# Attention beside a token MLP: loads awaited at other matrix products, the last four scores on other halves of the rows, and two pieces of set-up moved

## The chip, the cores and the metric

The kernel runs on one core of a Trainium2 chip, in one launch. Five engines work from queues of their own, each in order: PE (TensorE, matrix products), DVE (VectorE), ACT (ScalarE, here above all the exponentials), POOL (GpSimd) and SP (SyncE, which here issues DMA transfers). They meet through semaphores. The metric is the device time of one execution in microseconds (us).

## The reference

```python
def attention(x, wqkv, wo):          # x: 1 x 2048 x 512, 32 heads of 16
    qkv = (x @ wqkv).reshape(B, S, 3, H, Dh).transpose(2, 0, 3, 1, 4)
    q, k, v = qkv[0], qkv[1], qkv[2]
    p = softmax(einsum("bhqd,bhkd->bhqk", q, k) * Dh ** -0.5)
    o = einsum("bhqk,bhkd->bhqd", p, v)
    return o.transpose(0, 2, 1, 3).reshape(B, S, D) @ wo

def mixer(x, w1, b1, w2, b2):        # over the 2048 tokens, 1792 hidden
    u = gelu(einsum("bsd,sf->bdf", layernorm(x), w1) + b1)
    return (einsum("bdf,fs->bds", u, w2) + b2).transpose(0, 2, 1)

g = sigmoid((x * gate_w).sum(-1, keepdims=True))
return g * attention(x, wqkv, wo) + (1 - g) * mixer(x_B, w1, b1, w2, b2)
```

All in float32. The two branches have inputs of their own, A_x and B_x.

## The kernel before, in words

Most products of float32 values are made of three products of a rounded high part and a rest (names with `_hi` and `_lo`). Three stretches of the program follow one another: the projections, with q and k written to DRAM in parts; the first layer of the MLP with its gelu; and the attention, with the second layer of the MLP and the output projections running beside it. A short tail ends it. The change lies in the attention.

**Groups and phases.** The attention is 32 groups, each of a pair of heads and one half of the query rows; a group has 4 phases (`ph` 0 to 3), so there are 128 phases, counted by `p`. All engines follow the order in which the code is written here (`manual_schedule`).

**Scores.** A phase makes 16 scores (line 907), each a product of 64 rows (keys and queries in their parts, stacked; `ks` and `qs`) by 512 columns into a PSUM bank of its own, tiles `s` and, from score 10 on, `t`. A stack holds one head in rows 0 to 63 and the other in rows 64 to 127; `head[n]` says which half score `n` uses. A product on one half can run beside a product on the other half. So the first `n_b` scores of a phase share the array with a dense half product of the other branch (line 916, tile `dn`, also 64 rows); the scores from `n_b` on alternate between the halves and run beside each other. `n_b` is 14 in phases 0 to 91, 0 in phases 92 to 95, 12 in phases 96 to 111, and 6 or 8 from 112 on.

**Exponentials.** Scores 1, 3, 5 and 7 are copied out of PSUM by DVE (line 924, tile `pe`, four copies) and exponentiated together by ACT at the phase's end (line 939). Scores 0, 2, 4, 6, 8, 9 are exponentiated one by one straight from PSUM (line 928, "singles"), and (10, 11), (12, 13), (14, 15) two at a time (line 869; as two single ones on line 872 where their banks are not adjacent, in phase 0 of a group). There are 8 banks, one for dense products, so a late score waits for a bank that an earlier one must leave: score 14 awaits DVE's copy of score 7 and ACT's single of score 8.

**Products by v.** After the scores come the products of the exponentials by v (line 792, `apply_v`), as a rule 32 a phase, into a bank `av`. Each pair of scores that `TURNS` and `HELD` name gives four. The `pe` pairs, and where `whole` allows it the last pair, are `held` and applied in the next phase; in phase 0 the held ones finish the group before. A phase in which the last pair is held makes 28, the one after it more. DVE adds `av` to the group's sum `ot` (lines 814 and 816) early in the next phase, ahead of the four copies.

**Loads.** `load_q` (8 DMAs, phase 0) and `load_k` (6 DMAs, phase 1) bring the next group's stacks through `stack` (line 505) on SP's queue. No instruction awaits them but the next group's first scores: score 0 those of its half of the rows, and the first score on the other half, score 15 where `n_b` is 14, those of the other.

**Set-up.** `shift_rows` (line 492) sets 2 × 16 rows of a key buffer to −1, for the first buffer on POOL ahead of the attention and for the second on DVE in phase 0. `open_end`, called at phase 92, makes on DVE two constants for the end (`sums_of` and `least`, lines 589 to 596).

Of the kernel before, what the change touches and what calls it, by code (L numbers as in the profile page):

```python
# [9 lines left out]
F32 = mybir.dt.float32  # L10
# [4 lines left out]
ALU = mybir.AluOpType  # L15
AX = mybir.AxisListType
SYNC = mybir.DependencyInfo(mybir.DependencyClass.Sync, mybir.DependencyReason.DATA)
REASON = "the two halves of the rows add to one bank"
PSUM = bass.MemoryType.PSUM
DRAM = bass.MemoryType.DRAM  # L20

P = 128
# [36 lines left out]
def gated_mix(ctx: ExitStack, tc: tile.TileContext, a_x, a_wqkv, a_wo, b_w1, b_b1, b_w2, b_b2, gate_w, out):  # L59
    nc = tc.nc  # L60
# [435 lines left out]
        shift_rows(nc.gpsimd, k_bufs[0])  # L496


    def stack(dst, src, which, pair, cols, planes):
        b, r0 = divmod(pair * 2 * DH, P)  # L500
        for i in range(2):
            rows = slice(r0 + i * DH, r0 + (i + 1) * DH)
            for row, *part in planes:
                at = slice(i * HALF + row, i * HALF + row + DH)
                nc.sync.dma_start(dst[at].bitcast(F32), src[b][part[which], rows, cols])

    def load_k(g):
        t = k_bufs[g % 2]
# [56 lines left out]
    def call(at, *what):  # L565
        calls.setdefault(at, []).append(what)
# [14 lines left out]
    def open_end():  # L581

        nonlocal end, sums_of
        u_ctx.close()
        wk_ctx.close()
        end = end_ctx.enter_context(tc.tile_pool(name="end", bufs=1, side="right", reuse_waits="tile"))

        sums_of = end.tile([P, P], F32, name="sums_of")
        nc.vector.tensor_copy(
            sums_of.rearrange("p (j r) -> p j r", r=32),  # L590
            ident.rearrange("p (j r) -> p j r", r=32)[:, :, DH:VC].broadcast_to([P, P // 32, 32]),
        )
        least.append(end.tile([P, 1], F32, name="least"))
        nc.vector.tensor_reduce(least[0], ident.rearrange("p (j r) -> p j r", r=32)[:, :, DH], axis=AX.X, op=ALU.add)
        nc.vector.tensor_scalar(least[0], least[0], -1.0, 3e38, ALU.add, ALU.mult)
        nc.vector.tensor_scalar_add(least[0], least[0], LEAST_SUM)
# [129 lines left out]
            call(p0, invert, half, k, pairs, p0 + (0 if half and k > 1 else 2))  # L726
    p0 = 2 * at
    call(p0, open_end)
    left, right = slice(0, NB), slice(NB, QW)
    for k in range(ND):  # L730
        call(p0 + k // 2, fetch_half, k, left, p0 + 2 + k // 2, p0 + 2 + k // 2)
# [50 lines left out]
            dst = r_d[half][k][None, 2 * p : 2 * (p + 1), cols]  # L782
            nc.sync.dma_start(dst, ot[rows][DH:].rearrange("r (i n) -> r i n", i=2))

    def apply_v(av, grp, pairs, final=False):

        for n, pair in enumerate(pairs):
            for i, c, qb, pt in sorted(pair, key=lambda u: u[2]):
                for h in range(2):
                    j = 2 * qb + h  # L790
                    v_at = (c * H + grp % NP * 2 + i) * VC
                    nc.tensor.matmul(  # L792
                        av[32 * j : 32 * (j + 1), i * QC : (i + 1) * QC],
                        v_flat[:, v_at : v_at + 32],
                        pt[:, h * QC : (h + 1) * QC],
                        start=n == 0,
                        stop=n == len(pairs) - 1,
                    )
        covered = [{qb for pair in pairs for i, _, qb, _ in pair if i == n} for n in range(2)]
        assert all(len(c) != 1 for c in covered)  # L800
        if grp not in sums:
            sums[grp] = ot_pool.tile([P, NB], F32, name="ot"), [False, False]
        ot, begun = sums[grp]
        halves = [n for n in range(2) if covered[n]]
        if grp == NG - 1 and final:
            parts = [(x, y, True) for x, y in zip(column_halves(ot), column_halves(av))]
        elif len(halves) == 2 and begun[0] == begun[1]:
            parts = [(ot, av, begun[0])]
        else:
            cols = [slice(n * QC, (n + 1) * QC) for n in range(2)]  # L810
            parts = [(ot[:, cols[n]], av[:, cols[n]], begun[n]) for n in halves]
        for x, y, more in parts:
            if more:
                nc.vector.tensor_tensor(x, y, x, ALU.add)  # L814
            else:
                nc.vector.tensor_copy(x, y)
        for n in halves:
            begun[n] = True
        if final and grp < NG - 1:
            store(grp, sums.pop(grp)[0])  # L820

    engines = {getattr(mybir.EngineType, name) for name in ("PE", "Activation", "DVE", "Pool", "SP")}
    with tc.manual_schedule(engines=engines):
        kt, qt = {0: load_k(0)}, {0: load_q(0)}
        held, fence, turn, spare = [], None, 0, 0

        for n, (step, *args) in enumerate(first):
            if n and n % 12 == 0:
# [6 lines left out]
        for p in range(LAST + 1):  # L835
# [13 lines left out]
            half = slice(0, HALF) if second else slice(HALF, P)  # L849

            head = [second if n < n_b else (n - n_b) % 2 for n in range(NSC)]
            qbs = {}
            for a, b in TURNS + HELD:
                if head[a] == head[b]:
# [3 lines left out]
                    qbs[zero], qbs[one] = turn, 1 - turn  # L858
                    turn = 1 - turn

            swap = ph == PHASES - 1 and p < LAST and head[TWO[1][0]] == head[TWO[1][1]]
            order = [*TURNS[:4], TURNS[5], TURNS[4]] if swap else TURNS

            def exps(n):
# [14 lines left out]
            pool = regions()  # L879
            psum = pool.__enter__()  # L880
            ones = [psum.tile([P, NB], F32, name=f"s{n}") for n in range(BANKS)]
            for n in range(NSC):
                i, qb = head[n], qbs[n]
                c = at[i][qb]
                at[i][qb] += 1
                if n < TWO[0][0]:
                    if n >= BANKS:
                        ones[share[n - BANKS]] = psum.tile([P, NB], F32, name=f"s{share[n - BANKS]}")
                    s = ones[share[n % BANKS]]
                else:  # L890
                    if n == TWO[0][0]:
                        pool.__exit__(None, None, None)
                        pool = regions()
                        psum = pool.__enter__()
                        twos = {}
                        for low in range(BANKS):
                            if low == share[2]:
                                av = psum.tile([P, NB], F32, name="av")
                            elif low in share[3:5] and ph == 0:
                                twos[low] = psum.tile([P, NB], F32, name=f"s{low}")  # L900
                            elif low not in twos:
                                two = psum.tile([P, 2, NB], F32, name=f"t{low}")
                                twos[low], twos[low + 1] = two[:, 0, :], two[:, 1, :]
                                twos[low, low + 1] = two
                    s = twos[share[(n - BANKS) % BANKS]]
                rows_i = slice(i * HALF, i * HALF + ROWS)
                nc.tensor.matmul(  # L907
                    s,
                    kt[grp][rows_i, c * P : (c + 1) * P],
                    qt[grp][rows_i, qb * NB : (qb + 1) * NB],  # L910
                    start=True,
                    stop=True,
                )
                if n < n_b:
                    ps, a, b, begin, last, done = beside[n]
                    mm = nc.tensor.matmul(ps, a[half], b[half], start=begin and not second, stop=last and bool(second))  # L916
                    if n == 0 and fence is not None:
                        tc.add_manual_dep(mm.ins, fence.ins.name, SYNC, reason=REASON)
                    if n == n_b - 1:
                        fence = nc.gpsimd.memset(token, 0.0)  # L920
                        tc.add_manual_dep(fence.ins, mm.ins.name, SYNC, reason=REASON)
                if n in EVAC:
                    pt = evac[:, EVAC.index(n), :]
                    nc.vector.tensor_copy(pt, s)  # L924
                    units[n] = i, c, qb, pt
                elif n in SINGLE:
                    pt = ptp.tile([P, NB], F32, name="p1", bufs=len(SINGLE))
                    nc.scalar.activation(pt, s, AF.Exp, scale=SCALE)  # L928
                    units[n] = i, c, qb, pt
                else:  # L930
                    units[n] = i, c, qb, None
                    if n == TWO[0][1] or n == TWO[1][1] and not swap:
                        exps(n)
                    elif n == TWO[2][1]:
                        exps(n)
                        if swap:
                            exps(TWO[1][1])
# [2 lines left out]
            if n_b and second and beside[-1][-1]:  # L940
                beside[-1][-1]()
            if p == 0:
                shift_rows(nc.vector, k_bufs[1])
            if second:
                for _ in range(2):
                    if len(ready) < 2:
# [3 lines left out]

            turns, now_held = ([tuple(units[n] for n in pair) for pair in pairs] for pairs in (order, HELD))
            spare = share[2]
            if ph < PHASES - 1 or swap:

                def whole(pairs):
                    met = {(i, qb) for pair in pairs for i, _, qb, _ in pair}
# [9 lines left out]
                    av = psum.tile([P, NB], F32, name=f"s{spare}")  # L966
                apply_v(av, grp, turns)
            elif p < LAST:
                apply_v(av, grp, held + turns)
            else:  # L970
                ot = sums[grp][0]
                nc.vector.tensor_scalar_max(ot, ot, least[0])
                apply_v(av, grp, held + turns + now_held, final=True)
                last_ot = ot
# [165 lines left out]
```

## Time and profile before

| | |
|---|---|
| time, median of 3 runs | 1293.89 us (1293.07 to 1294.15) |
| the profiled execution | 1295.3 us; its span from first to last instruction 1293.3 us |
| mean granted clock of TensorE | 0.997 |
| busy: PE, ACT, DVE, POOL | 1280.4, 1091.3, 671.0, 180.0 us |
| attention, phases 0 to 127 | from 304.7 to 1273.7 us |

The profile comes from one execution. A table by stage gives, for a stretch in us from the span's start, its length and each engine's busy time, with the granted clock (1.00 is full) and the share of time in which the DMA engines were busy. A timeline row has start, length, engine, line, operation, and what the engine idled for ahead of it. PE's matrix products overlap in the pipeline, so the starts of rows say more than their lengths: a score's row is 0.39 or 0.50 us long, and the next begins 0.23 us after it.

### The profile page before, as it was taken

To read this page: it belongs to the slowest core of one execution; us is meant where nothing else is said; L and a number is where in the kernel's file an instruction comes from. 1 tells how busy PE (TensorE), PEld (TensorE's weight loads), DVE (VectorE), ACT (ScalarE), POOL (GpSimd) and SP (SyncE) were. 2 spreads that over 40 slices of the span, in tenths; PEclk is the share of its full clock that TensorE was granted. 3 is DMA by queue.
4 is the path that set the end of the run, shared out by engine and by line. 5 is a ranking of instruction groups with operands and counts; after the bars stand their busy time and mean duration, and the time that the engine had idled before them with its cause. 6 is when DMAs were issued, how large, how long until landed. Compare 5 with 4: busy or idle time off the path is not lost.

```text
span 1293.3 us, 33067 instructions
## 1 busy us (share of the span) xinstructions
PE 1280.4 (99%) x13278; PEld 850.4 (66%) x13278; DVE 671.0 (52%) x1155; ACT 1091.3 (84%) x1537; POOL 180.0 (14%) x272
## 2 busy tenths in 40 slices
PE   9999999999999999999999999999999999999997
PEld 7888888886666666666666666666665565655555
DVE  5675362438445545544544444454454665645555
ACT  3443343447999999999999999999999999999994
POOL 0210244553110111011011101101110000000000
PEclk9999999999999999999999999999999999999999
DMA  4497643327343343333334443333333654335411
GB/s 131 139 317 276 222 121 98 98 78 159 67 88 75 68 97 83 77 68 81 77 60 98 83 77 66 81 75 60 88 68 75 151 135 114 81 84 108 80 44 72
DMA packets 93581, 133.20 MB, mean 103 GB/s; under 512 B 16277, under 2 KB 55339, under 8 KB 90348
## 3 DMA queue, kind: packets, MB, share of 16 engines
q1 hardware_dynamic: 92844, 129.94, 41.2%
q8 instruction: 108, 1.77, 0.6%
q10 hardware_dynamic: 576, 1.05, 0.2%
q14 instruction: 53, 0.43, 0.1%
HBM read 97.00 MB, written 33.93 MB: 101 GB/s over the span
## 4 chain that ended last, share of the span: by engine, by line
PE 93%; ACT 4%; DVE 1%; issue 1%; DVEq 0%; ACTq 0%
PE av L792 28%; PE s L907 19%; PE acc L416 12%; PE t L907 10%; PE acc L73 10%; PE dn L916 6%; PE s L792 5%; ACT p L928 1%; ACT p L869 1%; ACT pe L939 1%; PE pa L996 1%; DVE pe L924 1%; PE acc L187 1%; PE dn L831 1%; PE acc L254 0%
## 5 line engine op out<-in xcount | busy, mean ns | idle before, releaser
L928 ACT ACTIVATE p<-s 128x512 f32<-128x512 f32 x768 | 395.7, 648 | 6.1 <-PE s L907 3.6
L869 ACT ACTIVATE p<-t 128x1024 f32<-128x1024 f32 x352 | 348.4, 1131 | 0.0
L907 PE MATMUL s<-qs,ks 64*128 64x512 f32 x1344 | 343.0, 404 | 1.1 <-DVE pe L924 0.7
L924 DVE COPY pe<-s 128x512 f32<-128x512 f32 x512 | 317.8, 683 | 6.9 <-PE s L907 6.4
L907 PEld LDWEIGHTS s<-qs,ks 64*128 64x128 f32 x1344 | 232.9, 184 | 97.5 <-issue 52.4
L792 PE MATMUL av<-p,v 128*32 128x256 f32 x4872 | 285.4, 379 | 0.0
L814 DVE TENSOR_TENSOR ot<-av,ot 128x512 f32<-128x512 f32 (+1 forms) x128 | 73.5, 575 | 396.6 <-PE av L792 396.6
L939 ACT ACTIVATE pe<-pe 128x2048 f32<-128x2048 f32 x129 | 259.5, 2014 | 0.0
L792 PEld LDWEIGHTS av<-p,v 128*32 128x32 f32 x4872 | 158.4, 110 | 104.9 <-issue 0.7
L907 PE MATMUL t<-qs,ks 64*128 64x512 f32 x704 | 185.1, 445 | 2.9 <-ACT p L928 0.4
L916 PE MATMUL dn<-u_lo,w_hi 64*128 64x512 f32 x430 | 174.1, 405 | 0.0
L916 PE MATMUL dn<-u_hi,w_lo 64*128 64x512 f32 x430 | 173.9, 404 | 0.0
L916 PE MATMUL dn<-u_hi,w_hi 64*128 64x512 f32 x428 | 173.2, 405 | 0.0
L66 POOL TENSOR_TENSOR w_lo<-w_raw,w_hi 128x512 fp32r<-128x512 f32 (+1 forms) x126 | 149.0, 1189 | 124.6 <-ACT w_hi L65 108.5
L907 PEld LDWEIGHTS t<-qs,ks 64*128 64x128 f32 x704 | 96.2, 184 | 83.4 <-ACT p L928 74.9
L792 PE MATMUL av<-pe,v 128*32 128x256 f32 x2048 | 138.1, 387 | 0.1
L920 POOL MEMSET token<- 1x1 f32 x124 | 12.7, 102 | 866.9 <-PE dn L916 811.2
L65 ACT CAST w_hi<-w_raw 128x512 fp32r<-128x512 f32 (+1 forms) x67 | 38.1, 569 | 79.2 <-PE acc L416 58.8
L792 PEld LDWEIGHTS av<-pe,v 128*32 128x32 f32 x2048 | 53.6, 109 | 54.2 <-ACT p L928 25.3
L416 PE MATMUL acc<-h_hi,w_hi 128*128 128x512 f32 x224 | 87.1, 389 | 0.0
L416 PE MATMUL acc<-h_lo,w_hi 128*128 128x512 f32 x224 | 87.1, 389 | 0.0
L416 PE MATMUL acc<-h_hi,w_lo 128*128 128x512 f32 x224 | 87.1, 389 | 0.0
(151 smaller groups left out, 1507.2 us busy)
## 6 DMA issues: line engine op xcount, KB each, us to landing
w_raw<-in_B_w_dram SPq DMA_DIRECT2D x96, 256.0 KB
ks<-kp SPq DMA_DIRECT2D x192, 128.0 KB
qs<-qp SPq DMA_DIRECT2D x256, 64.0 KB
qp<-pc SPq DMA_DIRECT2D x16, 768.0 KB
x<-in_A_x_dram SPq DMA_DIRECT2D x32, 256.0 KB
kp<-pc SPq DMA_DIRECT2D x16, 512.0 KB
w_raw<-in_B_w_dram SPq DMA_DIRECT2D x32, 128.0 KB
bp<-row SPq DMA_DIRECT2D x16, 256.0 KB
```

Of the source, the lines that this page charges most:

```text
L65: copy(hi, src)
L66: return sub(lo, src, hi.bitcast(F32), ALU.subtract)
L73: nc.tensor.matmul(ps, a, b, start=start and n == 0, stop=stop and n == last)
L416: nc.tensor.matmul(p, a, b, start=first and k == 0, stop=last and k == 2)
L792: nc.tensor.matmul(av[32 * j : 32 * (j + 1), i * QC : (i + 1) * QC], v_flat[:, v_at : v_at + 32], pt[:, h * QC : (h + 1) * QC], start=n == ...
L814: nc.vector.tensor_tensor(x, y, x, ALU.add)
L869: nc.scalar.activation(pt, twos[low, low + 1], AF.Exp, scale=SCALE)
L907: nc.tensor.matmul(s, kt[grp][rows_i, c * P : (c + 1) * P], qt[grp][rows_i, qb * NB : (qb + 1) * NB], start=True, stop=True,)
L916: mm = nc.tensor.matmul(ps, a[half], b[half], start=begin and not second, stop=last and bool(second))
L924: nc.vector.tensor_copy(pt, s)
L928: nc.scalar.activation(pt, s, AF.Exp, scale=SCALE)
L939: nc.scalar.activation(x, x, AF.Exp, scale=SCALE)
```

## The change

It has four parts.

1. The stack's DMAs of the next group are collected in `landed`. In a group's last phase (`ph` 3) `apply_v` makes each of 14 products by v, from the second pair on, wait for one of them.
2. Where `n_b` is 12 or less, which is phases 92 to 127, scores 12 and 13 use the first half of the rows and 14 and 15 the second, and they are issued in the order 12, 14, 13, 15. With 14 and 15 on one half their pair can always be held, so each of these phases makes 32 products by v.
3. The constants are made in `end_constants`, on DVE after the work of phase 101.
4. The second key buffer's shift rows are set by POOL.

```diff
@@ stack
+    landed = []
...
-                nc.sync.dma_start(dst[at].bitcast(F32), src[b][part[which], rows, cols])
+                landed.append(nc.sync.dma_start(dst[at].bitcast(F32), src[b][part[which], rows, cols]))
@@ open_end
         sums_of = end.tile([P, P], F32, name="sums_of")
+        least.append(end.tile([P, 1], F32, name="least"))
+
+    def end_constants():
+
         nc.vector.tensor_copy(
...
     call(p0, open_end)
+    on_dve(p0 + 9, end_constants)
@@ apply_v
-    def apply_v(av, grp, pairs, final=False):
+    def apply_v(av, grp, pairs, final=False, await_loads=False):
...
-                    nc.tensor.matmul(
+                    mm = nc.tensor.matmul(
...
+                    if await_loads and n and landed:
+                        tc.add_manual_dep(mm.ins, landed.pop(0).ins.name, SYNC, reason=AHEAD_OF_USE)
@@ the loop over phases
             head = [second if n < n_b else (n - n_b) % 2 for n in range(NSC)]
+            seq = list(range(NSC))
+            if n_b <= NSC - 4:
+                head[-4:] = 0, 0, 1, 1
+                seq[-3:-1] = seq[-2], seq[-3]
...
-            swap = ph == PHASES - 1 and p < LAST and head[TWO[1][0]] == head[TWO[1][1]]
+            swap = ph == PHASES - 1 and p < LAST and n_b == NSC - 2
...
-            for n in range(NSC):
+            for n in seq:
...
-                shift_rows(nc.vector, k_bufs[1])
+                shift_rows(nc.gpsimd, k_bufs[1])
...
-            if ph < PHASES - 1 or swap:
+            if ph < PHASES - 1 or swap or p < LAST and head[-2] == head[-1]:
...
-                apply_v(av, grp, held + turns)
+                apply_v(av, grp, held + turns, await_loads=ph == PHASES - 1)
```

How it moves instructions, at three places. First PE between group 0 and group 1, before: the last products of phase 3 and the first scores of phase 4 (a DMAHW semaphore is a load's).

```order
L792 MATMUL av<-p_3199,v 32x256 x2
L792 MATMUL av<-p_3213,v 32x256 [waits Activation_49]
L792 MATMUL av<-p_3213,v 32x256 x3
L792 MATMUL av<-p_3222,v 32x256 [waits Activation_49]
L792 MATMUL av<-p_3222,v 32x256 x3
L907 MATMUL s_3287<-qs,ks_2704 128x512 [waits DMAHW6_49,DMAHW1_49,DMAHW7_49,DMAHW0_49,PE_49]
L916 MATMUL dn<-u_hi,w_lo 128x512 [waits Pool_49]
```

The same place after, from the last two of the 14 awaited products on:

```order
L799 MATMUL av<-p_3178,v 32x256 [waits DMAHW3_49]
L799 MATMUL av<-p_3178,v 32x256 [waits DMAHW4_49]
L799 MATMUL av<-p_3185,v 32x256 x2
L799 MATMUL av<-p_3194,v 32x256 x2
L799 MATMUL av<-p_3199,v 32x256 x2
L799 MATMUL av<-p_3213,v 32x256 [waits Activation_49]
L799 MATMUL av<-p_3213,v 32x256 x3
L799 MATMUL av<-p_3222,v 32x256 [waits Activation_49]
L799 MATMUL av<-p_3222,v 32x256 x3
L921 MATMUL s_3287<-qs,ks_2704 128x512 [waits PE_49]
L930 MATMUL dn<-u_hi,w_lo 128x512 [waits Pool_49]
L921 MATMUL s_3288<-qs,ks_2704 128x512
```

Five waits ahead of the first score have become one; the loads are awaited one by one up in the products.

Then the end of phase 4's scores on PE, before; the last `t` row is score 15, the first on the other half of the rows.

```order
L907 MATMUL t_3334<-qs,ks_2704 128x512
L916 MATMUL dn<-u_hi,w_hi 128x512
L907 MATMUL t_3336<-qs,ks_2704 128x512 [waits DVE_49,Activation_49]
L907 MATMUL t_3336<-qs,ks_2704 128x512 [waits DMAHW4_49,DMAHW5_49,DMAHW3_49,DMAHW2_49]
L792 MATMUL av<-pe,v 32x256 [waits Activation_49]
L792 MATMUL av<-pe,v 32x256 x7
```

And after:

```order
L921 MATMUL t_3334<-qs,ks_2704 128x512
L930 MATMUL dn<-u_hi,w_hi 128x512
L921 MATMUL t_3336<-qs,ks_2704 128x512 [waits DVE_49,Activation_49]
L921 MATMUL t_3336<-qs,ks_2704 128x512
L799 MATMUL av<-pe,v 32x256 [waits Activation_49]
L799 MATMUL av<-pe,v 32x256 x7
```

Score 15's four waits for loads are gone; the rest stands as it did.

Last, phase 97 on PE, the last four scores and the first products, before (`t5` holds scores 12 and 13, `t1` 14 and 15):

```order
L907 MATMUL t5_14682<-qs_14040,ks0_2703 128x512 [waits DVE_49,Activation_49]
L907 MATMUL t5_14682<-qs_14040,ks0_2703 128x512
L907 MATMUL t1_14680<-qs_14040,ks0_2703 128x512 [waits DVE_49,Activation_49]
L907 MATMUL t1_14680<-qs_14040,ks0_2703 128x512
L792 MATMUL av_14679<-pe_14496,v_91 32x256 [waits Activation_49]
L792 MATMUL av_14679<-pe_14496,v_91 32x256 x7
```

After:

```order
L921 MATMUL t3_14673<-qs_14036,ks0_2703 128x512
L930 MATMUL dn_14487<-wo_hi_2735,e7_14159 128x512
L921 MATMUL t5_14674<-qs_14036,ks0_2703 128x512 [waits DVE_49,Activation_49]
L921 MATMUL t1_14672<-qs_14036,ks0_2703 128x512 [waits DVE_49,Activation_49]
L921 MATMUL t5_14674<-qs_14036,ks0_2703 128x512
L921 MATMUL t1_14672<-qs_14036,ks0_2703 128x512
L799 MATMUL av_14671<-pe_14488,v_91 32x256 [waits Activation_49]
```

Score 14, the first of the `t1` rows, with its wait for DVE and ACT, now stands ahead of score 13, the second of `t5`; score 15 still stands last.

More of the change, by code (lines that the diff above doesn't have):

```diff
@@ L17 @@
 SYNC = mybir.DependencyInfo(mybir.DependencyClass.Sync, mybir.DependencyReason.DATA)
+AHEAD_OF_USE = "the next group's scores find their stacks awaited"
 REASON = "the two halves of the rows add to one bank"
@@ L592, in open_end @@
         )
-        least.append(end.tile([P, 1], F32, name="least"))
         nc.vector.tensor_reduce(least[0], ident.rearrange("p (j r) -> p j r", r=32)[:, :, DH], axis=AX.X, op=ALU.add)
@@ L825, in gated_mix @@
         held, fence, turn, spare = [], None, 0, 0
+        landed.clear()
         for n, (step, *args) in enumerate(first):
```

## The prediction

> **What bounds the kernel now.** I read the page first: the busy shares, then the chain that ended last.
>
> ```profile
> span 1293.3 us, 33067 instructions
> PE 1280.4 (99%) x13278; PEld 850.4 (66%) x13278; DVE 671.0 (52%) x1155; ACT 1091.3 (84%) x1537; POOL 180.0 (14%) x272
> PE 93%; ACT 4%; DVE 1%; issue 1%; DVEq 0%; ACTq 0%
> PE av L792 28%; PE s L907 19%; PE acc L416 12%; PE t L907 10%; PE acc L73 10%; PE dn L916 6%; PE s L792 5%; ACT p L928 1%; ACT p L869 1%; ACT pe L939 1%; PE pa L996 1%; DVE pe L924 1%; PE acc L187 1%; PE dn L831 1%; PE acc L254 0%
> ```
>
> TensorE ends everything, but "busy" here includes scores that lie under something else's pace. So I cut the attention loop into its phases with the table by stage (columns: stretch and its length, busy time of each engine, granted clock, DMA share, GB/s). The sums are over groups 1 to 22, once over their first phases and once over their last; the single rows are phases 3, 4 and 24.
>
> ```profile
> 327.88:335.36 7.48, 7.48 (x98) 4.75 (x94) 3.71 (x7) 7.48 (x11) 2.10 (x3) 1.00 0.19 53
> 335.36:343.05 7.69, 7.69 (x98) 4.87 (x94) 3.60 (x6) 7.69 (x12) 0.09 (x1) 1.00 0.20 58
> 485.73:493.65 7.92, 7.92 (x98) 4.63 (x94) 4.63 (x8) 7.92 (x12) 0.09 (x1) 1.00 0.14 40
> sum 168.47, PE 168.47 PEld 106.59 DVE 81.23 ACT 168.47 POOL 1.96; mean PE 7.66 PEld 4.85 DVE 3.69 ACT 7.66 POOL 0.09
> sum 164.68, PE 164.68 PEld 103.83 DVE 88.01 ACT 164.68 POOL 34.04; mean PE 7.49 PEld 4.72 DVE 4.00 ACT 7.49 POOL 1.55
> ```
>
> A regular phase is 7.49 us; a group's first phase is 7.66. The timeline of TensorE at the end of the scores shows why (start, length): first a last phase, then the first phase of the next group.
>
> ```profile
> 331.34 0.50 PE L907 MATMUL t<-qs,ks 64*128 64x512 f32 x2
> 331.77 0.42 PE L792 MATMUL av<-pe,v 128*32 128x256 f32 x4
> ...
> 338.83 0.70 PE L907 MATMUL t<-qs,ks 64*128 64x512 f32 x2
> 339.46 0.64 PE L792 MATMUL av<-pe,v 128*32 128x256 f32 x8
> ```
>
> Scores 14 and 15 start together 3.46 us into the phase, and the products follow 0.43 later. In the group's first phase they start at 3.47 too, but take 0.70: score 15 is 0.20 late, and the products come 0.63 after. Ahead of score 15 stands there its wait for four loads. The products themselves last the same: 335.36 − 331.77 = 3.59 for 32 of them.
>
> What sets the 3.46 is VectorE; a late phase (96) shows it best.
>
> ```profile
> 1030.44 0.69 DVE L814 TENSOR_TENSOR ot<-av,ot 128x512 f32<-128x512 f32 x1 [1.24 <-PE av L792]
> 1031.14 2.48 DVE L924 COPY pe<-s 128x512 f32<-128x512 f32 x4
> 1033.77 0.51 PE L907 MATMUL t<-qs,ks 64*128 64x512 f32 x2
> 1034.20 1.07 PE L792 MATMUL av<-pe,v 128*32 128x256 f32 x16
> 1030.30:1037.79 7.49, 7.49 (x96) 4.67 (x92) 3.60 (x6) 7.36 (x12) 0.09 (x1) 1.00 0.65 174
> 1044.85:1052.61 7.76, 7.76 (x96) 4.37 (x93) 4.89 (x8) 7.76 (x11) 0.09 (x1) 1.00 0.92 146
> sum 120.89, PE 120.28 PEld 72.74 DVE 71.14 ACT 120.37 POOL 1.96; mean PE 7.52 PEld 4.55 DVE 4.45 ACT 7.52 POOL 0.12
> sum 113.48, PE 111.67 PEld 64.31 DVE 60.12 ACT 112.65 POOL 2.23; mean PE 7.44 PEld 4.29 DVE 4.01 ACT 7.51 POOL 0.15
> 1181.42:1189.23 7.81, 7.44 (x84) 4.07 (x81) 4.50 (x7) 7.51 (x12) 0.09 (x1) 1.00 0.14 32
> 1183.02 2.47 DVE L924 COPY pe<-s 128x512 f32<-128x512 f32 x4
> ```
>
> The sum and four copies end at 1033.62, 3.32 into the phase; score 14 needs the bank of the fourth copy and starts 0.15 later. The sums are phases 96 to 111 (mean 7.56) and 112 to 126 (7.57). Some of these phases hold 28 products and some 36; after a short one ScalarE is still behind (7.76 in phase 98).
>
> **The change part by part.**
>
> *Awaited loads.* Removed: the waits on loads at a group's first score and at score 15. The first score's cost nothing now, since the gap from products to scores is alike in all phases. Score 15's is 168.47 − 164.68 = 3.79 over 22 groups, less 0.27 for another stall of phase 24, which stays (7.92, against a mean of 160.55/21 = 7.65 of the rest): **−3.52**. Groups 23 and later are costed below. Added: 14 single waits, each on one product, 14 × 31. Those products run one after another at 3.59/32 = 0.112 us, and two of them carry a ScalarE wait today at no cost; so I take 0. From above: at what score 15's four waits cost, 0.20 or 0.05 each, they would be 0.7 us a group if none of it hides. Behind a waiting product stand on TensorE the other products and the next scores, then all engines. So it matters whether loads have landed.
>
> ```profile
> 1012.39 3.28 SPq L505 DMA_DIRECT2D ks<-kp x6
> 986.60:994.40 7.80, 7.80 (x101) 4.75 (x100) 3.46 (x6) 7.80 (x12) 0.18 (x2) 1.00 0.01 2
> 1015.01:1022.40 7.39, 7.33 (x84) 3.72 (x80) 6.52 (x11) 7.39 (x11) 0.00 (x0) 1.00 0.99 137
> ```
>
> For group 23 the DMA engines are idle (0.01) well before its products at 994.40. The tightest is group 24: its six key loads (0.77 MB) are issued until 1015.67 and at 137 GB/s would be in by 1021.3 (an estimate), the awaited products start at 1026.3: 0, at most the 3.6 us until the next group's scores, once. The Trainium skill, "DMA: Bandwidth & Descriptors", Rules for kernel authors, speaks against this edit: issue early and wait late, while here the wait moves earlier. By that rule the sum would carry up to those 3.6 us; no row here shows a late load.
>
> *Last four scores.* This touches phases 92 to 127. In the new order 12, 14, 13, 15, score 14 still awaits the fourth copy, 13 stands behind it on the other half of the rows and runs beside it, and 15 shares its half with 14 and comes alone. What one score behind another on the same half costs, from the start of phase 18:
>
> ```profile
> 440.72 0.50 PE L907 MATMUL s<-qs,ks 64*128 64x512 f32 x1
> ...
> 441.06 0.39 PE L907 MATMUL s<-qs,ks 64*128 64x512 f32 x1
> ```
>
> Score 15 starts 0.34 after 14 (the first of a run; 0.23 is the pace later). After a cold pair (0.50) the products came at 0.43; after a warm score (0.39) I take 0.11 less, 0.32. So the products start 0.34 + 0.32 − 0.43 = 0.23 later: 7.49 + 0.23 = **7.72** a phase. Bounds: 0.12 (pace 0.23) to 0.34 (0.43 kept). In return each phase gets 32 products, so that ScalarE, which falls back only after a phase of 28, is no bound. Sums: 16 × 7.72 = 123.52 against 120.89, **+2.63**; 15 × 7.72 = 115.80, plus 0.75 for phase 116, whose copies end 4.07 into it instead of 3.32 behind other VectorE work (1185.49 − 1181.42), 116.55 against 113.48: **+3.07**; phase 127, 0 to 0.23, **+0.1**.
>
> *Shift rows.*
>
> ```profile
> L492 POOL MEMSET ks<- x2: 1844/1906/1967, 300.4 to 302.4; 16x2048 f32 x2
> L492 DVE MEMSET ks<- x2: 1765/1765/1765, 309.4 to 311.6; 16x2048 f32 x2
> 313.40 0.42 DVE L816 COPY ot<-av 128x256 f32<-128x256 f32 x1
> 312.04:320.38 8.34, 8.17 (x99) 4.53 (x95) 5.29 (x8) 8.34 (x11) 1.38 (x2) 1.00 0.62 106
> 313.23 3.09 ACT L928 ACTIVATE p<-s 128x512 f32<-128x512 f32 x6
> 316.79 0.64 PE L792 MATMUL av<-pe,v 128*32 128x256 f32 x8
> ```
>
> In phase 1 (from 312.04) VectorE's sum waits for the memsets until 313.40. Without them it would start at 312.18, and VectorE alone would let the products start at +3.90 instead of +4.75. But ScalarE's singles end at 316.32, +4.28, and a product awaits the last of them; with 0.06 for the handing over the gain is 4.75 − 4.34: **−0.41** (0 to −0.85). On GpSimd they take 2 × 1.9 us; its next duty is the next phase's fence, and it is 14% busy.
>
> *Constants, phases 92 to 95.*
>
> ```profile
> 997.96:1007.62 9.66, 8.95 (x85) 4.10 (x82) 4.03 (x10) 8.35 (x12) 0.00 (x0) 0.82 0.61 136
> 1002.36:1005.77 3.41, 3.41 (x34) 1.57 (x36) 0.42 (x1) 3.41 (x4) 0.00 (x0) 0.50 0.53 103
> 998.71 0.22 DVE L589 COPY sums_of<-ident 128x128 f32<-128x128 f32 x1
> 999.29 2.48 DVE L924 COPY pe<-s 128x512 f32<-128x512 f32 x4
> sum 32.34, PE 31.37 PEld 15.52 DVE 20.14 ACT 30.44 POOL 0.00; mean PE 7.84 PEld 3.88 DVE 5.04 ACT 7.61 POOL 0.00
> ```
>
> The four constants hold the copies back by 0.58 (998.71 to 999.29). After, without dense work, such a phase is 7.39 (the row of 1015.01) + 0.23 = 7.62; four are 30.48 against 32.34: **−1.86**. In that lie 1.67 us of half clock: 3.41 us at 0.50, which is half lost. I count it as gone, since TensorE waits less ahead of it, but from rows I cannot show that. The Trainium skill, "TensorE: Matmul & The Clock Gate", Part 1, has a free-running window of 3413 ns whose low activity halves the clock; the 3.41 us agree, and by that rule the loss may come or not from run to run. In phase 101 the constants cost 0 to 0.6 once.
>
> *Sum.* −3.52 − 0.41 + 2.63 + 3.07 + 0.1 − 1.86 = 0.0 on the profiled execution, 1295.3 (span 1293.3 and 2.0 around it): 1295.3. That execution is 1.4 above the median of the runs, 1293.89, about the 1.67 of half clock; if the others lacked it, the sum for them is +1.7: 1295.6. I take **1295.4**.
>
> **The rivals.**
>
> *The last scores cost nothing (faster).* The rows of halves give the products their scores as early as before, and equal phases end ScalarE's backlog: phases stay at 7.49, and 7.39 without dense work. That is 16 × 7.49 = 119.84 (−1.05), 15 × 7.49 + 0.75 = 113.10 (−0.38), 4 × 7.39 = 29.56 (−2.78); with −3.52 and −0.41 it is −8.1: 1287.2. For it: 7.76 exists only behind ScalarE. Against: 13 can't pass 14 on an engine in order. Chance 0.18.
>
> *The tail is dearer (slower).* The lone score 15 drains like a cold one: 0.34 instead of 0.23 in 35 phases, +3.9: 1299.3. It decides from about 0.27 on. The pair at 338.83 speaks for it: there the products came 0.43 after the late score 15, though that one had waited. Chance 0.13.
>
> *The waits on products cost (slower).* 0.05 × 14 unhidden in 31 groups: +22, about 1317. It decides from some 0.1 us a group on. Against: the products' pace with ScalarE waits in it. Chance 0.06.
>
> *The clock halves all the same.* Nothing of the 1.67 is saved: 1297.1. Chance 0.13.
>
> That the waits merely reappear at score 15 would be a change that does not do what it says; its order shows none there.
>
> **How the numbers follow.** My forecast has 0.50 and on its own spans 1293.0 to 1298.0. The range, 1290.0 to 1299.0, leaves out the first rival's core and the dear waits. A difference of 0.2%, 2.6 us, is about what can be told from no change. Faster, below 1291.3: the first rival and the low end of the last scores' bounds, 0.20. Slower, above 1296.5: 0.13 + 0.06, most of the clock's 0.13 and the forecast's upper edge, 0.34. Between: 0.46.
>
> **What would show it.** First phases of groups 1 to 22 at 7.49, not 7.66; products of last phases still 3.59; late phases alike at 7.72, with score 15 alone at about 3.81 and products at 4.13; phase 1 at 7.9; no stretch at clock 0.50. Wrong if late phases are at 7.49 or under, or if the products with waits stretch.

## The result and the profile after

| | before | after |
|---|---|---|
| time, median | 1293.85 us (1292.61 to 1296.37, 14 runs) | 1295.65 us (1293.18 to 1298.57, 14 runs) |
| ratio to before | | 1.0013, 95% interval 1.0005 to 1.0022 |
| profiled execution, span | 1295.3, 1293.3 us | 1297.84, 1296.1 us |

The change makes the kernel slower by a little over 0.1%, inside what was called no change. From the page after, the span and the chain that ended last by engine:

```profile
span 1296.1 us, 32939 instructions
PE 95%; DMA 1%; ACT 1%; DVE 1%; issue 1%; SPq 1%; ACTq 0%
```

A DMA stands in the chain now, which it did not before. The table by stage shows where the time went: first the sums over the first, second and last phases of groups 1 to 22, then phases 1, 63, 95, 96 and 116, then the sums over phases 96 to 111 and 112 to 126.

```profile
sum 164.67, PE 164.67 PEld 103.01 DVE 81.24 ACT 164.59 POOL 1.94; mean PE 7.49 PEld 4.68 DVE 3.69 ACT 7.48 POOL 0.09
sum 165.42, PE 165.42 PEld 101.42 DVE 78.09 ACT 165.42 POOL 33.81; mean PE 7.52 PEld 4.61 DVE 3.55 ACT 7.52 POOL 1.54
sum 165.03, PE 165.03 PEld 101.98 DVE 88.03 ACT 165.03 POOL 33.99; mean PE 7.50 PEld 4.64 DVE 4.00 ACT 7.50 POOL 1.55
311.94:320.05 8.11, 7.93 (x99) 4.49 (x95) 4.09 (x7) 8.11 (x11) 2.35 (x3) 1.00 0.50 85
777.26:785.11 7.85, 7.85 (x98) 4.58 (x94) 3.71 (x7) 7.85 (x11) 2.09 (x3) 1.00 0.11 28
1017.60:1027.62 10.02, 9.49 (x84) 4.26 (x80) 6.52 (x11) 8.12 (x11) 0.00 (x0) 1.00 0.76 154
1027.62:1035.31 7.69, 7.56 (x96) 4.65 (x93) 3.60 (x6) 7.15 (x11) 0.09 (x1) 1.00 0.73 177
1181.37:1190.52 9.15, 7.95 (x92) 4.17 (x88) 5.17 (x8) 8.20 (x12) 0.09 (x1) 1.00 0.16 39
sum 123.00, PE 120.90 PEld 74.24 DVE 70.71 ACT 121.43 POOL 1.41; mean PE 7.56 PEld 4.64 DVE 4.42 ACT 7.59 POOL 0.09
sum 116.77, PE 112.00 PEld 64.20 DVE 60.17 ACT 114.48 POOL 2.22; mean PE 7.47 PEld 4.28 DVE 4.01 ACT 7.63 POOL 0.15
```

Added up for the two profiled executions:

| stretch | before | after | difference | predicted |
|---|---|---|---|---|
| up to phase 0 | 304.69 | 305.29 | +0.60 | 0 |
| phases 0 and 1 | 15.69 | 14.76 | −0.93 | −0.41 |
| first phases, groups 1 to 22 | 168.47 | 164.67 | −3.80 | −3.52 |
| second phases | 164.77 | 165.42 | +0.65 | 0 |
| last phases | 164.68 | 165.03 | +0.35 | 0 |
| phases 92 to 95 | 32.34 | 32.81 | +0.47 | −1.86 |
| phases 96 to 111 | 120.89 | 123.00 | +2.11 | +2.63 |
| phases 112 to 126 | 113.48 | 116.77 | +3.29 | +3.07 |
| phase 127 and the tail | 28.6 | 28.7 | +0.1 | +0.1 |
| span | 1293.3 | 1296.1 | +2.8 | 0.0 |

The timeline of TensorE shows the two main mechanisms at work: the end of the scores of phase 8, a group's first (start 365.00), and of phase 98 (start 1042.99).

```profile
368.47 0.50 PE L921 MATMUL t<-qs,ks 64*128 64x512 f32 x2
368.89 0.64 PE L799 MATMUL av<-pe,v 128*32 128x256 f32 x8
...
1046.47 0.50 PE L921 MATMUL t<-qs,ks 64*128 64x512 f32 x2
1046.78 0.39 PE L921 MATMUL t<-qs,ks 64*128 64x512 f32 x1
1047.10 1.07 PE L799 MATMUL av<-pe,v 128*32 128x256 f32 x16
```

In phase 8 scores 14 and 15 start together again, and the products follow at 3.89. In phase 98 they come at 4.11: scores 14 and 13 start together at 3.48 (the row of two), and score 15 runs alone behind them, from 3.79 on.

Phase 95 holds what was not counted. First TensorE's products of that phase, then SP's issues of group 24's key loads.

```profile
1021.60 1.07 PE L799 MATMUL av<-pe,v 128*32 128x256 f32 x16
1022.49 2.37 PE L799 MATMUL av<-p,v 128*32 128x256 f32 x16
1025.11 2.58 PE L799 MATMUL av<-p,v 128*32 128x256 f32 x32 [0.26 <-DMA ks<-kp]
...
1009.76 5.48 SPq L508 DMA_DIRECT2D ks<-kp  x6
```

A product by v shows as two records in these rows, so 64 are 32 products. They start at 1021.60 and would end 3.59 later, at 1025.19; the next score starts at 1027.62. They stand 2.43 us in all for loads issued from 1009.76 on.

### The profile page after: what moved, and what is told of

Same layout as the page of the kernel before. It is cut to its first block, busy times and chain, and to the rows that moved or that the text cites. A ratio compares the mean times of both kernels' runs of the same rounds, so it can differ in the third digit from the quotient of the medians.

```text
span 1296.1 us, 32939 instructions
## 1 busy us (share of the span) xinstructions
PE 1278.8 (99%) x13278; PEld 842.1 (65%) x13278; DVE 666.6 (51%) x1157; ACT 1091.7 (84%) x1537; POOL 182.6 (14%) x274
## 4 chain that ended last, share of the span: by engine, by line
PE 95%; DMA 1%; ACT 1%; DVE 1%; issue 1%; SPq 1%; ACTq 0%
PE av L799 30%; PE s L921 21%; PE t L921 12%; PE acc L417 12%; PE acc L74 10%; PE s L799 5%; PE dn L930 4%; DMA ks<-kp 1%; PE pa L1010 1%; ACT p L942 1%; PE acc L188 1%; PE dn L841 1%; DVE pe L938 0%; DMA x<-in_A_x_dram 0%; PE acc L255 0%
## 5 line engine op out<-in xcount | busy, mean ns | idle before, releaser
L942 ACT ACTIVATE p<-s 128x512 f32<-128x512 f32 x768 | 408.6, 748 | 7.3 <-PE s L921 3.9
L883 ACT ACTIVATE p<-t 128x1024 f32<-128x1024 f32 x352 | 361.7, 1234 | 0.0
L921 PE MATMUL s<-qs,ks 64*128 64x512 f32 x1344 | 339.1, 403 | 1.1 <-DVE ot L823 0.8
L799 PE MATMUL av<-p,v 128*32 128x256 f32 x4904 | 290.2, 379 | 0.3 <-DMA ks<-kp 0.3
L823 DVE TENSOR_TENSOR ot<-av,ot 128x256 f32<-128x256 f32 (+1 forms) x128 | 72.4, 566 | 399.6 <-PE av L799 399.6
L953 ACT ACTIVATE pe<-pe 128x2048 f32<-128x2048 f32 x129 | 273.0, 2118 | 0.0
L921 PEld LDWEIGHTS t<-qs,ks 64*128 64x128 f32 x704 | 92.0, 184 | 92.1 <-ACT p L942 89.5
```

The source lines that it names most:

```text
L799: mm = nc.tensor.matmul(av[32 * j : 32 * (j + 1), i * QC : (i + 1) * QC], v_flat[:, v_at : v_at + 32], pt[:, h * QC : (h + 1) * QC], start ...
L883: nc.scalar.activation(pt, twos[low, low + 1], AF.Exp, scale=SCALE)
L921: nc.tensor.matmul(s, kt[grp][rows_i, c * P : (c + 1) * P], qt[grp][rows_i, qb * NB : (qb + 1) * NB], start=True, stop=True,)
L953: nc.scalar.activation(x, x, AF.Exp, scale=SCALE)
```

## The experiments

Each part was done alone first, beside the changed kernel without one of its waits. The kernel before ran beside them (median 1293.0, 27 runs).

**Awaited loads alone.** On the kernel before, nothing else of the change:

```diff
+                landed.append(nc.sync.dma_start(...))
...
+                    if await_loads and n and landed:
+                        tc.add_manual_dep(mm.ins, landed.pop(0).ins.name, SYNC, reason=AHEAD_OF_USE)
...
-                apply_v(av, grp, held + turns)
+                apply_v(av, grp, held + turns, await_loads=ph == PHASES - 1)
```

> The kernel before with the awaited loads alone. Theory (three parts that act separately): the first phases of groups 1 to 22 fall from 7.66 to 7.48 us, the products of the last phases stay at 3.59, and the time is 3 to 3.5 us below before, about 1290.5. In phase 95 the products start at 1026.3 in the old rhythm, when the loads for group 24 have just landed: 0 to 0.5 us. Rival (a wait on a product costs like one at score 15, 0.05 each): the products of each last phase take 4.0 to 4.3 us and the time rises to some 1305 or more. Second rival (the loads for group 24 are late for any kernel that awaits them at products): phase 95 stands for about 2.4 us and the gain shrinks to about 1 us.

Measured: 1291.16 us (1288.8 to 1293.13, 11 runs), ratio 0.9984 (0.9975 to 0.9993). From its table by stage the first phases, the second ones and phase 95, and from its timeline the products that stood:

```profile
sum 165.05, PE 165.05 PEld 103.60 DVE 81.22 ACT 165.05 POOL 1.94; mean PE 7.50 PEld 4.71 DVE 3.69 ACT 7.50 POOL 0.09
sum 165.17, PE 165.17 PEld 101.81 DVE 78.05 ACT 165.17 POOL 33.89; mean PE 7.51 PEld 4.63 DVE 3.55 ACT 7.51 POOL 1.54
1017.43:1026.91 9.48, 8.72 (x92) 3.94 (x88) 6.52 (x11) 8.37 (x11) 0.00 (x0) 1.00 0.85 156
...
1023.86 3.12 PE L795 MATMUL av<-p,v 128*32 128x256 f32 x40 [0.56 <-DMA ks<-kp]
```

The time is 1.8 us below before in the medians, where 3 to 3.5 were expected. The first phases fall as forecast, so the waits on loads ahead of their scores were what made them longer. But phase 95 is 9.48 instead of 7.90 before, so the second rival holds in kind: without the new last four scores, too, a kernel that awaits group 24's loads at products stands for 1.6 us. That my theory gave 0 to 0.5 there was wrong; its timing came from an execution in which phase 92 lost 1.7 us at half clock. The dear waits are out: 14 waits cost nothing where the loads have landed, since the last phases sum to 164.72 here and to 164.68 before.

**Last four scores alone.** On the kernel before:

```diff
+            seq = list(range(NSC))
+            if n_b <= NSC - 4:
+                head[-4:] = 0, 0, 1, 1
+                seq[-3:-1] = seq[-2], seq[-3]
...
-            for n in range(NSC):
+            for n in seq:
...
-            if ph < PHASES - 1 or swap:
+            if ph < PHASES - 1 or swap or p < LAST and head[-2] == head[-1]:
```

> The kernel before with the new last four scores alone (halves, order and held pair in phases 92 to 127). Theory: phases 96 to 126 at 7.69 us each instead of a mean of 7.56, because score 15 comes alone 0.31 after score 14; +4 to +5 us over 31 phases, phases 92 to 95 about +0.2 each without a stretch at half clock; the time 1297.5 to 1299. Phase 95 does not stand, since no product awaits a load. Rival (the loss in the changed kernel was only its late loads in phases 95 and 116, and equal phases are no slower): within 1 us of before.

Measured: 1298.05 us (1297.14 to 1299.61, 5 runs), ratio 1.0042 (1.0028 to 1.0056). Its first phases, and its phases 96 to 111 and 112 to 126:

```profile
sum 168.44, PE 168.44 PEld 106.32 DVE 81.20 ACT 168.44 POOL 1.94; mean PE 7.66 PEld 4.83 DVE 3.69 ACT 7.66 POOL 0.09
sum 122.79, PE 120.87 PEld 74.08 DVE 70.13 ACT 121.99 POOL 1.41; mean PE 7.55 PEld 4.63 DVE 4.38 ACT 7.62 POOL 0.09
sum 116.22, PE 112.09 PEld 64.31 DVE 59.96 ACT 114.47 POOL 2.23; mean PE 7.47 PEld 4.29 DVE 4.00 ACT 7.63 POOL 0.15
```

The first phases stay at 7.66 and the late ones rise by 1.90 and 2.74. This part alone is a loss of 5 us, with no late load in it: phase 95 was 7.58.

**Set-up alone.** On the kernel before:

```diff
+    on_dve(p0 + 9, end_constants)
...
-                shift_rows(nc.vector, k_bufs[1])
+                shift_rows(nc.gpsimd, k_bufs[1])
```

> The kernel before with the constants and the shift rows moved alone. Theory: phases 0 and 1 together 0.9 us shorter (15.69 to about 14.8), phase 92 about 0.5 shorter, and no stretch at half clock there or less of one: 1.3 to 2 us below before, about 1292. Rival (what VectorE no longer does was hidden by ScalarE): at most 0.4 us.

Measured: 1292.0 us (1291.84 to 1293.15, 11 runs), ratio 0.9992 (0.9983 to 1.0001): too small to tell by time. Its phases 1 and 92:

```profile
311.72:319.92 8.20, 7.93 (x99) 4.54 (x95) 4.14 (x7) 8.20 (x11) 2.43 (x3) 1.00 0.63 116
997.57:1004.95 7.38, 7.24 (x85) 3.95 (x81) 3.50 (x6) 7.38 (x12) 0.00 (x0) 1.00 0.68 163
```

Phase 92 at 7.38 must be held against a phase 92 with the constants in it and without half clock. The kernel with awaited loads alone has one, and its phase 1 has the memsets on VectorE:

```profile
311.74:320.14 8.40, 8.15 (x98) 4.59 (x95) 5.35 (x8) 8.40 (x11) 1.37 (x2) 1.00 0.60 113
994.68:1002.66 7.98, 7.40 (x84) 3.62 (x80) 4.03 (x10) 7.98 (x12) 0.00 (x0) 1.00 0.73 175
```

So the constants were worth 0.60, and the shift rows 0.20 in phase 1. Of the 0.93 that phases 0 and 1 lost together, the rest is no merit of the move: phase 0 was 7.35 before but 6.57 in the kernel with awaited loads alone, where nothing of the set-up had moved.

**No awaits in phase 95.** The changed kernel with

```diff
-                apply_v(av, grp, held + turns, await_loads=ph == PHASES - 1)
+                apply_v(av, grp, held + turns, await_loads=ph == PHASES - 1 and p != 95)
+                if p == 95:
+                    landed.clear()
```

> The changed kernel, but in phase 95 alone no product awaits a load (the next group's scores do, as in the kernel before). Theory (loads for group 24 land at about 1025.1, in the middle of the products but ahead of the next scores): phase 95 falls from 10.02 to about 7.6 us, phase 96 hardly grows, and the time is 2 to 2.4 us below the changed kernel, about 1293.3. Rival (the wait only moves on to the first score of phase 96 or to its score 15): phase 96 grows by what phase 95 loses and the time is that of the changed kernel within 0.5 us.

Measured: 1294.09 us (1293.69 to 1297.64, 11 runs), ratio 1.0014 (1.0005 to 1.0023). Its phases 95 and 96:

```profile
1017.22:1024.80 7.58, 7.34 (x84) 3.86 (x81) 6.52 (x11) 7.58 (x11) 0.00 (x0) 1.00 0.76 140
1024.80:1032.43 7.63, 7.55 (x96) 4.62 (x92) 3.60 (x6) 7.63 (x12) 0.09 (x1) 1.00 0.77 224
```

In the profile the theory holds to the tenth: 2.44 us go from phase 95 and none come back in phase 96. In time it is not resolved: by the medians this run is 1.1 us above before and the changed kernel 1.8, and the ratios to before are the same, with intervals of ±0.9 in a thousand, or 1.2 us. The 2 to 2.4 us that were expected are not seen. That the stall costs 2.4 in every execution is therefore not shown; it was 2.43, 1.57 and, in the next experiment, 0.97.

The remaining three ran beside the kernel before at 1293.12 (23 runs).

**Plain order of the last four.** On the changed kernel:

```diff
                 head[-4:] = 0, 0, 1, 1
-                seq[-3:-1] = seq[-2], seq[-3]
```

> The changed kernel with its last four scores in plain order, 12, 13, 14, 15. Theory (what counts is that 14 and 15 share a half, so that 15 starts 0.31 after 14 whatever stands beside): late phases stay at 7.69 us, the time is the changed kernel's, about 1295.5. Rival (13 queued behind 14 is what costs): late phases fall to about 7.49 and the time by 6 us.

Measured: 1294.93 us (1294.14 to 1297.0, 11 runs), ratio 1.0016 (1.0007 to 1.0025). Its phases 96 to 111, and the end of the scores in phase 97 (start 1033.20):

```profile
sum 123.00, PE 123.00 PEld 76.07 DVE 70.70 ACT 121.45 POOL 1.41; mean PE 7.69 PEld 4.75 DVE 4.42 ACT 7.59 POOL 0.09
...
1035.86 1.51 PE L920 MATMUL t<-qs,ks 64*128 64x512 f32 x5
1037.30 0.42 PE L799 MATMUL av<-pe,v 128*32 128x256 f32 x4
```

The same sum, and 4.10 to the first product, as in the changed kernel (4.11 in phase 98). Score 13 behind 14 costs nothing; that 14 and 15 share a half is the price, and the last run below, where they do not share one, confirms it.

**The change without its last four scores.** Awaited loads (not in phase 95) and the set-up, on the kernel before.

> The kernel before with awaited loads (but not in phase 95) and with the set-up moved: the change without its last four scores. Theory (parts add up): first phases 7.49 with second ones some 0.03 longer, phase 95 at 7.9, phases 96 to 111 120.9 and 112 to 126 about 113.5 as before; about 4.3 us below the run without the awaits of phase 95 and 3.5 to 4 below before, near 1289.5. Rival (equal phases of 32 products were what kept ScalarE up, and the gain of the first phases is lost without them): within 1.5 us of before.

Measured: 1290.14 us (1289.54 to 1291.93, 11 runs), ratio 0.9980 (0.9971 to 0.9989). Phases 96 to 111:

```profile
sum 120.87, PE 119.96 PEld 72.14 DVE 71.65 ACT 120.36 POOL 1.93; mean PE 7.50 PEld 4.51 DVE 4.48 ACT 7.52 POOL 0.12
```

The time is 3.0 below before in the medians, where 3.5 to 4 were expected. That the parts add up holds by stage: the first phases keep their gain (164.65), which the rival denied, and phases 96 to 111 are as before. In time it is not shown so finely, since the interval reaches from 1.4 to 3.7 us.

**No pair held.** The kernel of the last experiment with

```diff
-            if ph < PHASES - 1 or swap:
+            if (ph < PHASES - 1 or swap) and n_b == NSC - 2:
```

so that phases 92 to 126 get equal numbers of products with scores 14 and 15 still on different halves (phase 92 has four more).

> As the change without its last four scores, and in phases 92 to 127 the last pair is never held for the next phase, so that these phases get 32 products each (36 in phase 92, 40 in phase 127) with scores 14 and 15 side by side as before. Theory (the phase is set by the four copies, scores 14 and 15 and the 32 products): late phases at 7.49 instead of a mean of 7.56, phases 96 to 111 119.9 and 112 to 126 about 112.9; 1 to 2 us below the kernel that holds, near 1288.3. Rival (the products of the last pair now wait for ScalarE's exponential of scores 14 and 15): the products of late phases take 3.7 to 4.0 instead of 3.59 and the time is 1 us or more above it.

Measured: 1289.04 us (1288.34 to 1289.94, 7 runs), ratio 0.9968 (0.9957 to 0.9979): the lowest median here. Phases 96 to 111 and 112 to 126, and the end of the scores in phase 98 (start 1039.77):

```profile
sum 119.95, PE 119.23 PEld 72.44 DVE 71.86 ACT 119.95 POOL 2.53; mean PE 7.45 PEld 4.53 DVE 4.49 ACT 7.50 POOL 0.16
sum 113.68, PE 110.10 PEld 63.91 DVE 60.10 ACT 112.98 POOL 2.22; mean PE 7.34 PEld 4.26 DVE 4.01 ACT 7.53 POOL 0.15
...
1042.76 0.97 PE L917 MATMUL t<-qs,ks 64*128 64x512 f32 x4
1043.66 0.64 PE L799 MATMUL av<-pe,v 128*32 128x256 f32 x8
```

The mean phase is 7.50; in phase 98 the products start at 3.89 and last 3.59 (the next phase starts at 1047.25), as the theory has it, so ScalarE's last pair comes in time. What the change sought with the new halves, equal phases, was to be had without them. The gain beyond the kernel that holds, 1.1 us in the medians, lies within the two intervals' reach and rests on the profile's 0.92 in phases 96 to 111; phases 112 to 126 give 0.16 (113.84 with the pair held), since phase 116 took 8.53 there.

## Why the prediction was right, point by point

**Awaited loads: right, with one bound that should have been a term.** The first phases gave 3.80 against 3.52, the difference being phase 24's stall, which left them. But for two (7.92 and 7.87) they had been of two kinds before, 7.57 to 7.59 and 7.68 to 7.71; the prediction shows only the second, but its sum counts both. The waits on products are free where loads have landed: the last phases sum to 165.03, 0.35 more than before, and that is phase 63 alone (7.85, 7.50 before). Two things were missed. The second phases took 0.65 more, 0.40 of it with the awaited loads alone (165.17 against the 164.77 of before): ScalarE is busy for all of the 165.42 now, and for 163.85 of the 164.77 before, so it probably falls behind in first phases of 7.49 instead of 7.66, and the second phase gives back 0.03. The rows fit this, though no run tests it alone: behind the 0.35 us that phase 63 stands, in which ScalarE can catch up, the second phases of the next six groups fall from about 7.53 to 7.48 to 7.50. And group 24's loads were priced at 0, at most 3.6; it was 2.43. The step that failed there was the timing of loads and products. The estimate of 1021.3 gave all of 137 GB/s to the loads, while the transfers around them shared it: from 1010.03 to 1025.11 the DMA engines moved some 2.1 MB (157 and 128 GB/s in the two halves), of which the loads are 0.77. And it took the products' start from an execution with a slow phase 92, where it lies 10.6 us behind the end of the loads' issue; in the changed kernel it lies 6.4 behind. The Trainium skill, "DMA: Bandwidth & Descriptors", Rules for kernel authors, has the rule that bears on this: issue a transfer early and wait on its semaphore late. Phase 95 agrees with it, 10.02 with the awaits and 7.58 without; where the loads had landed, in the other groups, waiting earlier cost nothing.

**Last four scores: right.** Predicted 7.72, measured 7.69, with products at 4.11 for 4.13 and score 15 at 3.79 for 3.81. Against it stood the rival that the scores cost nothing; the run with this part alone and the plain order put it out, and the dearer tail with it. The sums, +2.11 and +3.29 against +2.63 and +3.07, differ by 0.03 in each of 30 phases and by phase 116: 9.15, where 8.47 was expected. Its copies again stood behind VectorE's work on fetched rows, 0.71 longer than before (from 1.00 into the phase to 1.71). That work starts when such a row has landed: VectorE waits 2.29 us for it in phase 115, 1.81 before. So this phase hangs on a transfer and not on the scores alone; over the profiles here it was between 7.40 and 9.15.

**Shift rows: oversized.** −0.41 was taken, 0.20 is what phase 1 shows; phase 0's own spread hides it in the sum. The bound was the right one: in the changed kernel the products of phase 1 start at 316.46, 0.05 behind the end of ScalarE's singles. But that end was taken over at 4.28 into the phase, and it came at 4.47.

**Constants: right.** 7.63, 7.59 and 7.57 for the first three phases against 7.62, and phase 101, which now makes them, at 7.68 like its neighbours. Without the stall phases 92 to 95 sum to 30.38 (30.37 in the run without the awaits of phase 95) against 30.48.

**Half clock: gone from the profile; that the change did it is not shown.** None of the other profiled executions shows it in phases 92 to 95, not even those with the constants in place (7.98 at 1.00 with the awaited loads alone). The reason I gave, that TensorE waits less ahead of it, holds as far as it goes, but does not suffice. In the stretch from 1.04 to 4.40 us of phase 92 TensorE was busy for 2.65 of 3.36 us before, with the half clock behind it, and for 3.33 in the changed kernel. With the last four scores alone it was busy for 2.60 there, and the clock stayed full. The timed runs do not bear out a saving either: a mean granted clock of 0.997 or less, as the profiled execution before had, is on record in 4 of the 14 runs of the changed kernel and in 8 of the 50 of the kernel before that ran beside the experiments (these 8 took 1.4 to 1.7 us longer than the rest); where in those runs the clock was low is not known. The Trainium skill, "TensorE: Matmul & The Clock Gate", Part 1, says that its window runs free. That one profiled execution of nine had the loss in phase 92 agrees with it.

**The sum.** 1295.4 against 1295.65, and +1.7 against +1.8 where no half clock is saved. The two large terms came out nearly as sized (−3.80 and +5.40 for −3.52 and +5.70), but the match is better than its working: that forecast and median lie 0.25 us apart is partly luck. Between the two profiled executions the difference is +2.8 for 0.0: a stall of 2.43, a give-back of 0.65, 0.7 in phase 116 and 0.6 ahead of phase 0 were not in it. (The last lies in a stretch that the change does not touch, and which ended between 304.5 and 305.3 over the nine profiles.) The timed runs show less of this: the changed kernel's profiled execution lies 2.2 above their median. How much of the stall in phase 95 they carry stays open, since taking its waits away did not move the time by more than the intervals.

## What to carry to other kernels

A wait that an instruction already needs is free on an earlier one only as far as the data have landed there: look up the landing in the worst stage, not in the typical one, and leave the wait late where transfers crowd. When two changes each even out or pair up work, check which shared unit the pairing used: equal phases were worth 0.06 us each here, but score 15 without a partner cost 0.2. Do the parts of a change alone before taking a sum near zero for no effect; here −1.8 and +5.0 (with −1.0, not resolved, from the set-up) hid in +1.8.

## What the runs showed of the hardware

A stall of some 0.35 us stood in phase 24 of the kernels with the set-up in its old place (7.92 before) and in phase 63 of all with the set-up moved (7.85 after). It moves with the program; its cause stays open. Four waits for landed loads ahead of one score cost 0.1 or 0.2 us, by the group (first phases of 7.57 to 7.71 before, 7.48 to 7.50 after); one wait on each of fourteen products cost nothing that the profile shows. A score on the same half of the rows as the one ahead of it, with nothing beside it, started 0.31 us later, and this cost each phase 0.2 us.
